# Attention and experts on one core: the opening's sums, softmax steps and load order are rearranged

## The chip, the core and the metric

One core of a Trainium2 chip runs the program. The metric is device time in microseconds (us), the median of several runs. An engine's instructions run in the order in which the program lists them; engines wait for each other by semaphores only. SP (SyncE) is a queue that issues transfers. TensorE is PE, and its weight loads are PEld; VectorE is DVE, ScalarE is ACT, GpSimd is POOL.

## What is computed

For 8 batches of 8 heads (576 tokens, 64 wide) a softmax of `phi` over 32 memory slots turns keys and values into 32 slots each; queries attend to them. The 4608 x 512 result goes to eight experts, one for each token.

```python
a = softmax(phi - max(phi))                  # over 32 slots
k_m = einsum('bhsm,bhsd->bhmd', a, k)        # and v_m with v
attn = softmax(q @ k_m.T / 8)
x = attn @ v_m                               # heads side by side: 512 wide
logits = x @ w_gate + modality_bias[modality_id]
e = argmax(logits)
out = gate_w * (relu(x @ w1[e]) @ w2[e])     # w1: 512 x 1024, w2: 1024 x 512
```

## The kernel before

The kernel guesses one expert for all tokens from the first token's modality, computes with that, and at the end tests whether a token wanted another. Every float32 operand of a long product is split into an upper and a lower part (names end in `h` and `l`), and three products of parts stand for one. The product of attention weights and values with `w1` is reordered: the 32 values of a head are multiplied with `w1` first (`vwh`, `vwl`, line 776), and attention weights (`xah`, `xal`) are multiplied with that (`hidden`, line 831); `outputs` (line 868) multiplies with `w2`.

This case is about batch 0's opening, all that runs before that stream of long products fills PE.

- `phi` of batch 0 comes in two halves, one from ACT's queue and one from SP's (lines 1331 and 1332). `first_max` (line 310) takes maxima on DVE, PE turns them, `mem_top` reduces them to `topc` (line 324). Four small DVE instructions (lines 219 to 225) choose the guessed expert; SP reads the number (line 226) and issues the loads of `w1` in two halves, `raw1`, with `load_rest` (small tables `mid` and `wg`) between them (lines 228 to 232).
- `mem_exp` subtracts the peak (DVE, line 375) and takes exponentials (ACT, line 378). `first_products` (line 433) multiplies them with keys and then with values on PE. DVE adds the exponentials up over the nine token columns meanwhile (lines 389 to 392), and eight small products (line 444) add over partitions.
- `first_divide` forms reciprocals (DVE, lines 453 to 457) and ACT scales the even heads (line 470); `first_odd` adds the odd ones (line 477); PE turns the keys (line 150, `first_keys`), which needs the product of values to be issued before it. `first_scores` (line 593) gives scores.
- Softmax goes by head groups g = 0 and 1: turn (line 624), max (628), subtract (630), exponential (632), sum and scaling (666 to 669), turn (673), then `first_split` makes `xah` (ACT, 679) and `xal` (DVE, 681).
- `value_products` multiplies values with the first half of `w1`, twice (line 776); `value_rest` subtracts the upper part from the second copy on PE (line 790). Then comes the second half of `w1` ("0, 1"), and then the products `ha` to `he` of `hidden` for the first four of eight 128-column pieces: `ha` needs `xah` of group 0, `hb` its `xal`, `hc` needs `vwl`, `hd` and `he` need group 1. The other four pieces and `outputs` follow.

`plan_first` lists these steps by hand. `weave` then merges the list with the experts' steps: it simulates time with the costs in `TAKES` (first number PE's us; D, A, P, T for the engines), takes the next listed step when what it depends on is done in that simulation, and takes experts' products otherwise. The listed order is kept, so a listed step that has to wait holds back all listed after it. At `("start",)` the simulated time is set to 25. `prepare` and `biases` (POOL, lines 271 to 286) work out the bias that `add_logits` (line 728) adds before `gate`; its result scales the output rows (line 881). POOL also forms the lower parts of `w2` (line 924).

Of the kernel before, what the change touches and what calls it, by code (L numbers as in the profile page):

```python
# [54 lines left out]
def attn_moe(ctx: ExitStack, tc: tile.TileContext, q, k, v, phi, mod_id, w_gate, mod_bias, w1, w2, out):  # L55
# [28 lines left out]
    BUSY = 64, 10  # L84
# [23 lines left out]
    places = const.tile([P, 2], F32, name="places")  # L108
    busy = const.tile([P, 512], BF16, name="busy")
# [112 lines left out]
    def guess():  # L222

        nc.vector.tensor_reduce(row[:, 0:1], live.pop("mine"), axis=AX.X, op=ALU.max)
        nc.vector.tensor_scalar(star, row[:, 0:1], -1.0, float(E), op0=ALU.mult, op1=ALU.add)
        e = nc.sync.value_load(star[0:1, 0:1], min_val=0, max_val=E - 1)
        first = w1[bass.ds(e, 1)].rearrange("a (c p) f -> (a p) c f", p=P)
        for hf in range(2):
            cols = slice(hf * 512, (hf + 1) * 512)
            nc.sync.dma_start(raw1[:, :, cols], first[:, :, cols])  # L230
            if hf == 0:
                load_rest()
        second = w2[bass.ds(e, 1)].rearrange("a (c p) d -> (a p) c d", p=P)
        raw = stage_pool.tile([P, W2N, DM], F32, name="raw2")
        nc.sync.dma_start(raw, second[:, 0:W2N])
        live["raw2"] = [raw[:, c] for c in range(W2N)]

        for c in range(W2N, FCH):
            if c < FCH - 1:
                raw = wk.tile([P, DM], F32, name="ob", bufs=2)  # L240
            else:
                raw = wk.tile([P, HG, 4 * M], F32, name="t2sums").rearrange("p h x -> p (h x)")
            nc.sync.dma_start(raw, second[:, c])
            live["raw2"].append(raw)
        load_queries(0, RA, RB)
        load_phi(1)

    def load_rest():
        nc.sync.dma_start(
            mid[0:QP].rearrange("p b c t -> p b (c t)"),  # L250
            mod_id.bitcast(I32).rearrange("(b p c t) -> p b (c t)", b=B, c=QC, t=2),
        )
        nc.sync.dma_start(wg, w_gate.rearrange("(a p) e -> p a e", p=P))
# [127 lines left out]
    def mem_sums(b):  # L381
        pe = live["pe", b][0]
        if b == 0:
            x = pe.rearrange("p j x -> p (j x)")
            n = QC // 3 * P
            t2 = wk.tile([P, HG, 4 * M], F32, name="t2top").rearrange("p j x -> p (j x)")[:, 0:n]
            r = wk.tile([P, HG, M], F32, name="sums", bufs=2)
            rf = r.rearrange("p j m -> p (j m)")
            nc.vector.tensor_tensor(t2, x[:, 0:n], x[:, n:2 * n], op=ALU.add)
            nc.vector.tensor_tensor(t2, t2, x[:, 2 * n:3 * n], op=ALU.add)  # L390
            nc.vector.tensor_tensor(rf, t2[:, 0:P], t2[:, P:2 * P], op=ALU.add)
            nc.vector.tensor_tensor(rf, rf, t2[:, 2 * P:3 * P], op=ALU.add)
            live["pe", b] = pe, r
            return
        live["pe", b] = pe, fold(nc.gpsimd, pe, ALU.add, "sums", "sums")
# [25 lines left out]
    def first_products(t):  # L421
# [5 lines left out]
        if t == 0:  # L427
            live["sums0"] = pk[:, :, 2 * D]
# [10 lines left out]
    def first_sums():  # L439
        sums = live["pe", 0][1]  # L440
        for g in range(NG):
            for j in range(0, HG, 2):
                half = slice(QP * g, QP * (g + 1))
                nc.tensor.matmul(
                    live["first", 0][g][M * j:M * (j + 2), 2 * D:2 * D + 1],
                    lhsT=sums[half, j:j + 2].rearrange("p j m -> p (j m)"), rhs=ones_c[half],
                    start=True, stop=True, tile_position=(QP * g, M * j),
                )
# [134 lines left out]
    def first_scores(c0, n):  # L583

        sc = [pair_of_banks(g) for g in range(NG)]
        qT = q_sb[0].rearrange("p j (c u t) -> p j c u t", u=2, t=BL)
        cs = slice(c0, c0 + n)
        for u in range(2):
            for j in range(HG):
# [21 lines left out]
    def soften(b, part, step=None, groups=None):  # L611
# [8 lines left out]
        for gs in groups_of(b, part) if groups is None else [slice(groups, groups + 1)]:  # L620
# [8 lines left out]
            if step in (None, 2):  # L629
                nc.vector.tensor_tensor(x, x, m.broadcast_to(list(x.shape)), op=ALU.subtract)  # L630
# [44 lines left out]
    def first_split(g, step):  # L675
        h, l = (x[:, 0, g].rearrange("p c x -> p (c x)") for x in xa)
        src = live["aT", 0][:, g, 0:RA * QP]
        if step == 0:
            nc.scalar.copy(h, src)
        else:  # L680
            nc.vector.tensor_tensor(l, src, h.bitcast(F32), op=ALU.subtract)
# [244 lines left out]
    def first_w2(c):  # L926
# [68 lines left out]
    def plan_first():  # L995
# [26 lines left out]
        add(("max", 0), "max0", [], first_max, floor=4.5)  # L1022
        add(("top", 0), "top0", [("max", 0)], mem_top, 0)
        add(("preferred",), "guess", [], preferred)
# [14 lines left out]
        add(("s", 0, 0), "s0", [("kT", 0), ("qt", 0, 0, 1)], first_scores, 0, RA)  # L1039
# [3 lines left out]
        add(("prepare",), "nothing", [], prepare)  # L1043
        add(("bias", 0), "nothing", [], biases, 0)
# [3 lines left out]
        for k in range(2):  # L1048
            add(("e", 0, 0, 1, k), "e1", [], soften, 0, 0, k, 1)
        add(("n", 0, 0, 0, 0), "n1", [("e", 0, 0, 0, 3)], first_weights, 0, 0)  # L1050
        add(("n", 0, 0, 0, 1), "n2", [], first_weights, 0, 1)
        add(("e", 0, 0, 1, 2), "e1", [], soften, 0, 0, 2, 1)
        add(("vw", 0, 0), "vwp", [("kvT", 0)], value_products, 0, 0, pair_(0))
        add(("vwu", 0, 0), "vwu", [("vw", 0, 0)], value_upper, 0)
        add(("vw", 0, 2), "vwp", [], value_products, 0, 0, None, True)
        add(("xu", 0, 0, 0), "xu1", [("n", 0, 0, 0, 1)], first_split, 0, 0)
        add(("e", 0, 0, 1, 3), "ee", [("e", 0, 0, 1, 2)], soften, 0, 0, 3, 1)
        add(("xl", 0, 0, 0), "e1", [("xu", 0, 0, 0)], first_split, 0, 1)
# [8 lines left out]
        add(("vwu", 0, 1, 0), "vw1", [("vw", 0, 1)], value_upper, 1, range(1))  # L1067
        add(("n", 0, 0, 1, 1), "n2", [], first_weights, 1, 1)
        add(("xu", 0, 0, 1), "xu1", [("n", 0, 0, 1, 1)], first_split, 1, 0)
        add(("vwu", 0, 1), "vw1", [("vw", 0, 1)], value_upper, 1, range(1, 2))  # L1070
# [9 lines left out]
        add(("s", 0, 1), "s1", [("qt", 0, 1, 1), ("vwl", 0, 1)], first_scores, RA, RB, floor=28.6)  # L1080

# [247 lines left out]
    with tc.manual_schedule():  # L1329
        mid0 = wk.tile([1, 2], I32, name="mid0")  # L1330
        for half, eng in ((slice(HG // 2, HG), nc.scalar), (slice(0, HG // 2), nc.sync)):
            eng.dma_start(phs[0][:, half], halves(phi, 0)[:, half])
# [11 lines left out]
        nc.gpsimd.memset(ones_c, 1.0)  # L1344
        ones_r = wk.tile([1, P], F32, name="ones_r")
# [138 lines left out]
```

## Time and profile before

| | us |
|---|---|
| median of 3 runs (lowest and highest) | 381.92 (380.41, 382.25) |
| the profiled execution, its own time | 380.38 |
| its span, first to last instruction | 378.6 |
| PE busy in it | 370.4 |
| DVE, ACT, POOL busy | 248.6, 139.7, 46.1 |

The span starts at 0; a row's first number is its start. An instruction's record on PE includes its depth in the pipeline, so records of successive products overlap, and the spacing of the starts is what counts.

### The profile page before, as it was taken

How to read it: one execution, taken by the hardware profiler on the slowest of the kernel's cores; microseconds unless marked ns; L12 is line 12 of the kernel's file. 1: busy time of each engine (PE TensorE's matmuls, PEld its weight loads, DVE VectorE, ACT ScalarE, POOL GpSimd, SP SyncE). 2: the span in 40 equal slices, each digit the busy share in tenths (PEclk: the TensorE clock that was granted, in tenths of full speed). 3: DMA queues.
4: the chain of work that ended last, by engine and by line, in shares of the span. 5: the costliest groups of instructions: out<-in, count | busy, mean ns of one | idle time of the engine just before them, and what ended most of it. 6: DMA issues, size and time to landing. Idle time of an engine off the chain costs nothing.

```text
span 378.6 us, 9983 instructions
## 1 busy us (share of the span) xinstructions
PE 370.4 (98%) x4045; PEld 308.5 (81%) x4045; DVE 248.6 (66%) x618; ACT 139.7 (37%) x328; POOL 46.1 (12%) x110
## 2 busy tenths in 40 slices
PE   6899999999999999999999999999999999999996
PEld 2677887889878898898987889797987979697986
DVE  4788758885958797868855689567874538750400
ACT  2382433524344054323415244431623306240401
POOL 3148030022130030004000030004000000000000
PEclk9999999999999999999999999999999999999999
DMA  8999668969969547583653737760232102321112
GB/s 290 348 377 239 110 121 250 292 114 304 282 113 287 216 72 141 155 311 61 110 167 99 270 70 128 214 205 2 56 110 74 29 2 55 119 64 30 30 35 56
DMA packets 93979, 56.89 MB, mean 150 GB/s; under 512 B 69732, under 2 KB 75108, under 8 KB 93924
## 3 DMA queue, kind: packets, MB, share of 16 engines
q1 hardware_dynamic: 93648, 55.87, 53.9%
q8 instruction: 33, 0.54, 0.6%
q10 hardware_dynamic: 276, 0.30, 0.2%
q14 instruction: 22, 0.18, 0.2%
HBM read 37.28 MB, written 18.87 MB: 148 GB/s over the span
## 4 chain that ended last, share of the span: by engine, by line
PE 88%; DVE 5%; DMA 3%; ACT 2%; issue 1%; SPq 1%; ACTq 0%; DVEq 0%
PE pe L868 48%; PE pe L831 26%; PE pair L408 4%; DMA raw<-in_moe_w_dram 2%; PE pe L776 2%; PE pair L571 2%; PE pe L912 2%; PE pair L776 1%; PE pair L713 1%; DMA ph<-in_phi_dram 1%; DVE vwl L156 1%; PE pair L150 1%; DVE top L310 1%; DVE a L650 0%; DVE sa L640 0%
## 5 line engine op out<-in xcount | busy, mean ns | idle before, releaser
L868 PE MATMUL pe<-w2h,hh 128*128 128x512 f32 x280 | 111.3, 397 | 0.0
L868 PE MATMUL pe<-w2h,hl 128*128 128x512 f32 x280 | 109.4, 391 | 0.0
L868 PE MATMUL pe<-w2l,hh 128*128 128x512 f32 x280 | 107.2, 391 | 0.0
L848 DVE SCALAR_TENSOR_TENSOR hl<-pe,hh 128x256 fp32r<-128x256 f32 (+2 forms) x158 | 56.7, 389 | 35.3 <-ACT hh L844 34.6
L844 ACT ACTIVATE hh<-pe 128x256 fp32r<-128x256 f32 (+2 forms) x158 | 52.5, 361 | 33.2 <-PE pe L831 32.6
L868 PEld LDWEIGHTS pe<-w2h,hh 128*128 128x128 f32 x280 | 52.6, 188 | 11.9 <-DVE vwl L156 0.8
L868 PEld LDWEIGHTS pe<-w2l,hh 128*128 128x128 f32 x280 | 52.5, 188 | 11.2
L868 PEld LDWEIGHTS pe<-w2h,hl 128*128 128x128 f32 x280 | 52.7, 188 | 9.8
L881 ACT ACTIVATE ob<-pe,gates 128x512 f32<-128x512 f32 x35 | 23.9, 688 | 68.6 <-PE pe L868 40.2
L831 PE MATMUL pe<-xbh,vwh 128*128 128x320 f32 x128 | 40.3, 314 | 0.1
L831 PE MATMUL pe<-xbh,vwl 128*128 128x320 f32 x128 | 39.6, 309 | 0.0
L831 PE MATMUL pe<-xbl,vwh 128*128 128x320 f32 x128 | 39.6, 309 | 0.0
L831 PE MATMUL pe<-xah,vwh 128*128 128x256 f32 x124 | 35.3, 287 | 0.4 <-DVE hl L848 0.4
L831 PE MATMUL pe<-xal,vwh 128*128 128x256 f32 x124 | 34.9, 283 | 0.0
L831 PE MATMUL pe<-xah,vwl 128*128 128x256 f32 x124 | 34.9, 283 | 0.0
L831 PEld LDWEIGHTS pe<-xah,vwh 128*128 128x128 f32 x124 | 23.6, 192 | 2.7 <-ACT vwl L793 0.8
L831 PEld LDWEIGHTS pe<-xbh,vwh 128*128 128x128 f32 x128 | 24.0, 188 | 1.4 <-issue 0.5
L344 POOL COPY ts<-tm 32x4 f32<-32x4 f32 x24 | 5.0, 210 | 165.2 <-DVE tm L336 164.4
L831 PEld LDWEIGHTS pe<-xbl,vwh 128*128 128x128 f32 x128 | 24.1, 188 | 0.3
L831 PEld LDWEIGHTS pe<-xbh,vwl 128*128 128x128 f32 x128 | 24.0, 188 | 0.0
L831 PEld LDWEIGHTS pe<-xal,vwh 128*128 128x128 f32 x124 | 23.7, 192 | 0.2
L831 PEld LDWEIGHTS pe<-xah,vwl 128*128 128x128 f32 x124 | 23.7, 192 | 0.0
(178 smaller groups left out, 465.5 us busy)
## 6 DMA issues: line engine op xcount, KB each, us to landing
out_dram<-ob SPq DMA_DIRECT2D x72, 128.0 KB, 2.4
q_sb<-in_q_dram SPq DMA_DIRECT2D x112, 72.0 KB, 3.1
kv_sb<-in_k_dram SPq DMA_DIRECT2D x6, 1152.0 KB, 6.4
kv_sb<-in_v_dram SPq DMA_DIRECT2D x6, 1152.0 KB, 9.2
ph<-in_phi_dram SPq DMA_DIRECT2D x13, 288.0 KB, 8.1
kv_sb<-in_k_dram SPq DMA_DIRECT2D x4, 576.0 KB, 5.6
kv_sb<-in_v_dram SPq DMA_DIRECT2D x4, 576.0 KB, 6.1
raw<-in_moe_w_dram SPq DMA_DIRECT2D x2, 1024.0 KB, 7.8
```

Source lines behind the costliest of these rows:

```text
L150: nc.tensor.transpose(dst, src, ident[:rows, :rows])
L156: nc.vector.tensor_tensor(l, src, h.bitcast(F32), op=ALU.subtract)
L344: nc.gpsimd.tensor_copy(ts_[BL * a:BL * (a + 1)], live["tm"][BL * o:BL * (o + 1)])
L408: nc.tensor.matmul(live["kvp"][M * j:M * (j + 1), g], lhsT=pe[half, j, c * M:(c + 1) * M], rhs=kv_sb[half, :, j, c * D:(c + 1) * D], start ...
L571: nc.tensor.matmul(sc[g][M * j:M * (j + 1), a, 0:QC * BL], lhsT=kvT[b][rows, 0, M * j:M * (j + 1)], rhs=qT[rows, j, a], start=True, stop=T ...
L776: nc.tensor.matmul(pvs[g][M * j:M * (j + 1), :], lhsT=vT[b][rows, j, :], rhs=raw1[rows, j, cols], start=True, stop=not more, tile_position ...
L831: nc.tensor.matmul(ph[:, 0:n], lhsT=(vl if k == 2 else vh)[:, g, cols], rhs=xl if k == 1 else xh, start=(g == k == 0), stop=(g == NG - 1 a ...
L844: nc.scalar.activation(hs[0][:, f, h0:h0 + p1 - p0], live["ph", f][:, p0:p1], AF.Relu)
L848: nc.vector.scalar_tensor_tensor(hl, live["ph", f][:, p0:p1], 0.0, hh.bitcast(F32), op0=ALU.max, op1=ALU.subtract)
L868: nc.tensor.matmul(po, lhsT=tile_columns(hl if n == 1 else hh, f, t), rhs=(w2l if n == 2 else w2h)[:, f, :], start=(f == n == 0), stop=(f ...
L881: nc.scalar.activation(ob, po, AF.Copy, scale=gate_of(b, t))
L912: nc.tensor.matmul(po, lhsT=x, rhs=w2s[w][:, f, cols], start=(f == i == 0), stop=(f == FCH - 1 and i == 2),)
```

## The change

- The order of the first loads: both halves of `phi` go out on SP's queue, before keys; ACT's queue starts with the first token's modality and the bias row.
- `load_rest` loses `wg` and leaves the place between the halves of `w1`; `wg` goes ahead of the next batch's `phi`, `mid` behind it.
- DVE's four additions and the eight small products go. Nine products on PE take their place (`first_sums`): each has 128 columns of exponentials as its weights and moves two columns (`groups`, zeros and ones).
- `preferred` (two of the four small DVE instructions) comes ahead of `mem_top`.
- `first_odd` comes ahead of both query turns; scores of batch 0 come in two steps, two heads each.
- The subtraction of group 1 and the forming of `xal` of group 0 move from DVE to POOL.
- The four products `ha` come ahead of the second half of `value_products`; group 1's weights stand earlier in the list than that half.
- `prepare` and `biases` move behind the last step on `w2`.
- 56 small warm-up products in place of 64.

```diff
-    BUSY = 64, 10
+    BUSY = 56, 10
+    groups = const.tile([P, NG], F32, name="groups")
 def guess():
             nc.sync.dma_start(raw1[:, :, cols], first[:, :, cols])
-            if hf == 0:
-                load_rest()
 ...
         load_queries(0, RA, RB)
+        nc.sync.dma_start(wg, w_gate.rearrange("(a p) e -> p a e", p=P))
         load_phi(1)
+        load_rest()
 def load_rest():
 ...
-        nc.sync.dma_start(wg, w_gate.rearrange("(a p) e -> p a e", p=P))
 def mem_sums(b):
-        if b == 0:
 ...
-            nc.vector.tensor_tensor(t2, x[:, 0:n], x[:, n:2 * n], op=ALU.add)
-            nc.vector.tensor_tensor(t2, t2, x[:, 2 * n:3 * n], op=ALU.add)
-            nc.vector.tensor_tensor(rf, t2[:, 0:P], t2[:, P:2 * P], op=ALU.add)
-            nc.vector.tensor_tensor(rf, rf, t2[:, 2 * P:3 * P], op=ALU.add)
 def first_products(t):
-            live["sums0"] = pk[:, :, 2 * D]
+            live["sums0"] = pk[:, 0, 2 * D:2 * D + NG]
 def first_sums():
-        for g in range(NG):
-            for j in range(0, HG, 2):
-                nc.tensor.matmul(live["first", 0][g][M * j:M * (j + 2), 2 * D:2 * D + 1], ...)
+        pe = by_rows(live["pe", 0][0])
+        for c in range(QC):
+            nc.tensor.matmul(
+                live["sums0"], lhsT=pe[:, c].rearrange("p j m -> p (j m)"), rhs=groups,
+                start=(c == 0), stop=(c == QC - 1),
+            )
 def first_scores(c0, n, js=range(HG)):
-            for j in range(HG):
+            for j in js:
 def soften(b, part, step=None, groups=None):
-                nc.vector.tensor_tensor(x, x, m.broadcast_to(list(x.shape)), op=ALU.subtract)
+                eng = nc.gpsimd if b == part == 0 and groups else nc.vector
+                eng.tensor_tensor(x, x, m.broadcast_to(list(x.shape)), op=ALU.subtract)
 def first_split(g, step):
-            nc.vector.tensor_tensor(l, src, h.bitcast(F32), op=ALU.subtract)
+            (nc.vector if g else nc.gpsimd).tensor_tensor(l, src, h.bitcast(F32), op=ALU.subtract)
 TAKES
-    "first sums": (0.0, "T1.9")     "s0": (0.75, "")
+    "ks0": (0.4, "")     "s0h": (0.4, "")     "e1p": (0.0, "P0.55")
 plan_first
+        add(("preferred",), "guess", [], preferred)
         add(("top", 0), "top0", [("max", 0)], mem_top, 0)
-        add(("preferred",), "guess", [], preferred)
 ...
-        add(("sums", 0), "first sums", [("exp", 0)], mem_sums, 0)
-        add(("ks", 0), "nothing", [("sums", 0)], first_sums)
-        add(("kn", 0), "kn0", [("k", 0), ("sums", 0)], first_divide)
+        add(("ks", 0), "ks0", [], first_sums)
+        add(("kn", 0), "kn0", [("ks", 0)], first_divide)
+        add(("ko", 0), "ko0", [("kn", 0)], first_odd, 0)
         turns(0, 0, 9.5)
-        add(("ko", 0), "ko0", [("kn", 0)], first_odd, 0)
         turns(0, 1, 11.0)
 ...
-        add(("s", 0, 0), "s0", [("kT", 0), ("qt", 0, 0, 1)], first_scores, 0, RA)
+        add(("s0", 0), "s0h", [("kT", 0), ("qt", 0, 0, 0)], first_scores, 0, RA, range(2))
+        add(("s", 0, 0), "s0h", [("s0", 0), ("qt", 0, 0, 1)], first_scores, 0, RA, range(2, HG))
 ...
-        add(("prepare",), "nothing", [], prepare)
-        add(("bias", 0), "nothing", [], biases, 0)
 ...
+        add(("n", 0, 0, 1, 0), "n1", [("e", 0, 0, 1, 3)], first_weights, 1, 0)
+        add(("n", 0, 0, 1, 1), "n2", [], first_weights, 1, 1)
+        some_hidden("ha", "h0c", [("xu", 0, 0, 0)], range(1), range(1))
         add(("vw", 0, 1), "vwp", [], value_products, 0, 1, pair_(0))
-        add(("n", 0, 0, 1, 0), "n1", [("e", 0, 0, 1, 3)], first_weights, 1, 0)
-        some_hidden("ha", "h0c", [("xu", 0, 0, 0)], range(1), range(1))
 ...
         add(("s", 0, 1), "s1", [("qt", 0, 1, 1), ("vwl", 0, 1)], first_scores, RA, RB, floor=28.6)
+        add(("prepare",), "nothing", [("w2", FCH - 1)], prepare)
+        add(("bias", 0), "nothing", [], biases, 0)
 the start of the program
-        for half, eng in ((slice(HG // 2, HG), nc.scalar), (slice(0, HG // 2), nc.sync)):
-            eng.dma_start(phs[0][:, half], halves(phi, 0)[:, half])
+        for half in (slice(0, HG // 2), slice(HG // 2, HG)):
+            nc.sync.dma_start(phs[0][:, half], halves(phi, 0)[:, half])
```

## Rows read from the trace of the kernel before

**Rows 1.** The page's first part: busy us of each engine, its share of the span, and instructions.

```profile
PE 370.4 (98%) x4045; PEld 308.5 (81%) x4045; DVE 248.6 (66%) x618; ACT 139.7 (37%) x328; POOL 46.1 (12%) x110
```

**Rows 2.** The chain of work that ended last, in order of time, its first 25 us. The columns are start, us, and what.

```profile
0.74 3.92 DMA ph<-in_phi_dram
...
4.68 2.18 DVE top L310 x2
...
7.33 0.29 DVE topc L324
...
8.29 0.47 DVE exp L375
...
11.41 8.40 DMA raw<-in_moe_w_dram
...
19.95 1.89 PE pair L776 x16
```

**Rows 3.** PE's products in order of time (start, us from the first start to the last end, line, out<-in, count; in brackets the idle time before and what ended it).

```profile
14.36 0.44 PE L150 MATMUL pair<-ident,keys 128*128 128x128 f32 x2
...
16.94 1.09 PE L776 MATMUL pair<-raw,kvT 64*32 64x512 f32 x16 [0.35 <-ACT kvT L539]
17.82 1.07 PE L776 MATMUL pe<-raw,kvT 64*32 64x512 f32 x16
18.82 0.94 PE L790 MATMUL pe<-vwh,minus 128*128 128x512 f32 x2
...
24.73 0.28 PE L831 MATMUL pe<-xah,vwh 128*128 128x256 f32 x1
```

**Rows 4.** PE's weight loads in order of time. 64*64 or 128*128 is the part of the array that is loaded (rows * columns).

```profile
8.73 0.29 PEld L258 LDWEIGHTS pair<-row,ones_r 1*128 1x128 f32 x2 [0.57 <-issue]
9.36 1.95 PEld L433 LDWEIGHTS pair<-kv_sb,exp 64*64 64x64 f32 x72 [0.33 <-ACT exp L378]
11.73 0.21 PEld L444 LDWEIGHTS pair<-ones_c,sums 64*64 64x64 f32 x8 [0.42 <-DVE sums L392]
11.84 1.72 PEld L433 LDWEIGHTS pe<-kv_sb,exp 64*64 64x64 f32 x59
13.77 0.42 PEld L433 LDWEIGHTS pe<-kv_sb,exp 64*64 64x64 f32 x13 [0.21 <-issue]
14.36 0.20 PEld L150 LDWEIGHTS pair<-ident,keys 128*128 128x128 f32 x2 [0.17 <-issue]
...
20.78 0.14 PEld L776 LDWEIGHTS pair<-raw,kvT 64*32 64x32 f32 x4 [0.67 <-issue]
```

**Rows 5.** PE's weight loads of the first 26 us, grouped by form: busy us and mean ns of one.

```profile
L258 PEld LDWEIGHTS pair<-row,ones_r 1*128 1x128 f32 x2 | 0.3, 184 | 0.6 <-issue 0.6
...
L150 PEld LDWEIGHTS pair<-ident,keys 128*128 128x128 f32 x2 | 0.2, 140 | 0.2 <-issue 0.2
```

**Rows 6.** DVE in order of time.

```profile
8.14 0.14 DVE L225 TENSOR_SCALAR star<-row 1x1 int32<-1x1 f32 x1
...
12.09 0.16 DVE L453 TENSOR_SCALAR den<-pair 128x2 f32<-128x2 f32 x1 [0.41 <-PE pair L444]
...
13.30 0.86 DVE L477 SCALAR_TENSOR_TENSOR keys<-pair,recs,even 128x64 f32<-128x64 f32 x4
...
20.52 0.42 DVE L681 TENSOR_TENSOR xal<-aT,xah 128x256 fp32r<-128x256 f32 x1
...
21.63 0.42 DVE L669 TENSOR_TENSOR a<-a,ra 128x256 f32<-128x256 f32 x1
...
33.89 0.96 DVE L630 TENSOR_TENSOR a<-a,mx 128x640 f32<-128x640 f32 x1
```

**Rows 7.** ACT in order of time.

```profile
20.08 0.41 ACT L679 CAST xah<-aT 128x256 fp32r<-128x256 f32 x1 [0.87 <-DVE aT L673]
```

**Rows 8.** Stretches of one us: from, to, its length, then busy us and instructions of PE, PEld, DVE, ACT and POOL, the granted TensorE clock, the busy share of the 16 DMA engines, GB/s.

```profile
14.00:15.00 1.00, 0.80 (x16) 0.39 (x8) 0.78 (x2) 0.16 (x1) 0.00 (x0) 1.00 1.27 217
...
19.00:20.00 1.00, 0.82 (x8) 0.28 (x12) 0.93 (x4) 0.21 (x1) 0.92 (x3) 1.00 1.03 375
```

**Rows 9.** Transfers issued in the first 5 us: queue, size, us from issue to landing.

```profile
ph<-in_phi_dram ACTq DMA_DIRECT2D x1, 288.0 KB, 4.2
ph<-in_phi_dram SPq DMA_DIRECT2D x1, 288.0 KB, 3.9
```

**Rows 10.** POOL in order of time, the first 50 us.

```profile
17.09 0.35 POOL L271 CAST mid_f<-mid 64x16 f32<-64x16 int32 x2 [9.68 <-DMA mid<-in_moe_modality_id_dram]
...
19.82 0.34 POOL L286 TENSOR_TENSOR bias<-bias,part 128x72 f32<-128x72 f32 x1
...
32.86 1.31 POOL L924 TENSOR_TENSOR w2l<-ob,w2h 128x512 fp32r<-128x512 f32 x1
34.12 1.89 POOL L924 TENSOR_TENSOR w2l<-t2sums,w2h 128x512 fp32r<-128x512 f32 x1
...
49.75 0.74 POOL L299 TENSOR_TENSOR t2sums<-t2sums 128x256 f32<-128x256 f32 x1
```

**Rows 11.** The chain that ended last, 40 to 44 us.

```profile
40.77 0.19 DVE lg L728
...
42.45 0.70 ACT ob L881
...
43.19 0.85 PE pe L831 x4
```

More of the change, by code (lines that the diff above doesn't have):

```diff
@@ L382, in mem_sums @@
         pe = live["pe", b][0]
-        if b == 0:
[L384 to L388, printed above, removed]
-            nc.vector.tensor_tensor(t2, x[:, 0:n], x[:, n:2 * n], op=ALU.add)
-            nc.vector.tensor_tensor(t2, t2, x[:, 2 * n:3 * n], op=ALU.add)
-            nc.vector.tensor_tensor(rf, t2[:, 0:P], t2[:, P:2 * P], op=ALU.add)
-            nc.vector.tensor_tensor(rf, rf, t2[:, 2 * P:3 * P], op=ALU.add)
-            live["pe", b] = pe, r
-            return
         live["pe", b] = pe, fold(nc.gpsimd, pe, ALU.add, "sums", "sums")
@@ L439, in first_sums @@
     def first_sums():
-        sums = live["pe", 0][1]
-        for g in range(NG):
-            for j in range(0, HG, 2):
[L443 to L448, printed above, removed]
+        pe = by_rows(live["pe", 0][0])
[4 more added lines that the diff above has]
+            )
     def first_divide():
@@ L581, in scores, with first_scores @@
             load_queries(b + 2)
-    def first_scores(c0, n):
-        sc = [pair_of_banks(g) for g in range(NG)]
+    def first_scores(c0, n, js=range(HG)):
+        sc = [pair_of_banks(g) for g in range(NG)] if js[0] == 0 else live["sc", 0]
         qT = q_sb[0].rearrange("p j (c u t) -> p j c u t", u=2, t=BL)
@@ L1049, in plan_first @@
             add(("e", 0, 0, 1, k), "e1", [], soften, 0, 0, k, 1)
+        add(("e", 0, 0, 1, 2), "e1p", [("e", 0, 0, 1, 1)], soften, 0, 0, 2, 1)
         add(("n", 0, 0, 0, 0), "n1", [("e", 0, 0, 0, 3)], first_weights, 0, 0)
         add(("n", 0, 0, 0, 1), "n2", [], first_weights, 0, 1)
-        add(("e", 0, 0, 1, 2), "e1", [], soften, 0, 0, 2, 1)
         add(("vw", 0, 0), "vwp", [("kvT", 0)], value_products, 0, 0, pair_(0))
         add(("vwu", 0, 0), "vwu", [("vw", 0, 0)], value_upper, 0)
+        add(("e", 0, 0, 1, 3), "ee", [("e", 0, 0, 1, 2)], soften, 0, 0, 3, 1)
         add(("vw", 0, 2), "vwp", [], value_products, 0, 0, None, True)
         add(("xu", 0, 0, 0), "xu1", [("n", 0, 0, 0, 1)], first_split, 0, 0)
-        add(("e", 0, 0, 1, 3), "ee", [("e", 0, 0, 1, 2)], soften, 0, 0, 3, 1)
-        add(("xl", 0, 0, 0), "e1", [("xu", 0, 0, 0)], first_split, 0, 1)
+        add(("xl", 0, 0, 0), "e1p", [("xu", 0, 0, 0)], first_split, 0, 1)
         add(("vwr", 0, 0), "vwr", [("vwu", 0, 0)], value_rest, 0)
@@ L1061, in plan_first @@
             add(("vwl", 0, 0, g), "vw1", [("vwr", 0, 0)], value_remainder, 0, g)
+        add(("n", 0, 0, 1, 0), "n1", [("e", 0, 0, 1, 3)], first_weights, 1, 0)
+        add(("n", 0, 0, 1, 1), "n2", [], first_weights, 1, 1)
+        some_hidden("ha", "h0c", [("xu", 0, 0, 0)], range(1), range(1))
         add(("vw", 0, 1), "vwp", [], value_products, 0, 1, pair_(0))
-        add(("n", 0, 0, 1, 0), "n1", [("e", 0, 0, 1, 3)], first_weights, 1, 0)
-        some_hidden("ha", "h0c", [("xu", 0, 0, 0)], range(1), range(1))
         some_hidden("hb", "h0c", [("xl", 0, 0, 0)], range(1, 2), range(1))
         some_hidden("hc", "h0c", [("vwl", 0, 0, 0)], range(2, 3), range(1))
-        add(("vwu", 0, 1, 0), "vw1", [("vw", 0, 1)], value_upper, 1, range(1))
-        add(("n", 0, 0, 1, 1), "n2", [], first_weights, 1, 1)
         add(("xu", 0, 0, 1), "xu1", [("n", 0, 0, 1, 1)], first_split, 1, 0)
-        add(("vwu", 0, 1), "vw1", [("vw", 0, 1)], value_upper, 1, range(1, 2))
+        for g in range(NG):
+            add(("vwu", 0, 1, g) if g == 0 else ("vwu", 0, 1), "vw1", [("vw", 0, 1)], value_upper, 1, range(g, g + 1))
         add(("w2", 0), "w2", [], first_w2, 0)
@@ L1344, in attn_moe @@
         nc.gpsimd.memset(ones_c, 1.0)
+        for g in range(NG):
+            for r in range(NG):
+                nc.gpsimd.memset(groups[QP * r:QP * (r + 1), g:g + 1], float(g == r))
         ones_r = wk.tile([1, P], F32, name="ones_r")
```

4 rows, old and new, of the table TAKES are left out of this document.

## The prediction

> **What bounds the kernel now.** The page's first part comes first [rows 1]: PE is busy in 370.4 of 378.6 us, so a change pays only where PE waits, and most of that is in the opening. The chain of waits, in order of time, says what the opening is made of [rows 2]: `phi` lands at 4.66, DVE takes maxima until 6.86, `topc` ends at 7.62, the first subtraction starts at 8.29, and the second half of `w1` lands at 19.81, upon which PE starts that half's products at 19.95. That last link invites a misreading. In PE's order of time the product before it ends at 18.82 + 0.94 = 19.76 [rows 3], so the load costs PE 0.19 us and no more; a second chain, through softmax, arrives just as late. `xah` of group 0 is ready at 20.08 + 0.41 = 20.49 [rows 7]. From 19.95 PE is dense: 16 products with `w1` and 24 of `hidden` until, at 24.73, the other four pieces begin [rows 2, 3]. I take 24.73 as the mark: behind it PE runs products back to back, and what the mark moves, the end moves.
>
> **Front of the opening: 0.6 us gained.** The two halves of `phi` now come one behind the other on one queue. They landed at 0.74 + 3.9 and 0.73 + 4.2 [rows 9], sharing the engines, and both maxima waited for the first. Alone, the first should land earlier by about half of what the other half adds; DVE needs 2.18 / 2 = 1.09 for each [rows 2], so the second half has that long to come. I take 0.5. Bounds: nothing (both still land at 4.65), and 0.9 (the second half lands at 4.9, and 4.9 + 1.09 = 6.0 in place of 6.86). `preferred` moves into PE's turn of the maxima, and only `guess` stays between `topc` and the subtraction, beside PE's spreading of the peak. Of the 8.29 - 7.62 = 0.67 us there [rows 2] most is that spreading; I take 0.1, between nothing and 0.3. `preferred` is a new wait ahead of `mem_top` on DVE, for the modality's bias; that came behind half of `phi` on ACT's queue and now comes first, so I book nothing; if it were late, the 0.5 would go.
>
> **The sums: 1.4 us lost.** The additions that go are on DVE, not on PE. From the first load for keys at 9.36 to the first for values at 11.84 PE's load stream takes 2.48 [rows 4]: 72 loads in 1.95, a wait of 0.42 for DVE's sums, eight small loads in 0.11. Wait and small loads go: -0.53. In their place stand nine float32 products of two passes each, the two instructions that line 258 also shows for one product, so 18 loads of the whole 128 x 128 array. No row shows such a stream; the nearest: 64 x 64 loads come 1.95 / 72 = 0.027 apart [rows 4], and one whole array is four of them, 0.108; line 258's two loads of 128 columns take 0.29 together and 0.184 each, so 0.11 apart [rows 4, 5]. These agree, and I take 18 x 0.107 = 1.93. Low end: the two turns of keys load 128 x 128 at 0.20 together and 0.140 each, 0.06 apart [rows 4, 5], which gives 1.08; the planner's own cost in the diff, 0.4, is lower still. I stay with line 258, since its two loads are passes of one ordinary product and a turn is another instruction. So -0.53 + 1.93 = +1.4 (low ends +0.55 and -0.13).
> The Trainium skill weighs in on the other side: "TensorE: Matmul & The Clock Gate", Back-to-back issue gap, puts products of up to 64 columns at about 25 ns each once the clock is up. By that alone 18 take an estimated 0.45 and the step would be a small gain; line 258's spacing speaks against it, and its own case is below.
>
> What waits for it: `first_divide` starts later (12.09 before [rows 6]), but the turn of the keys at 14.36 [rows 3] comes behind the products of values on PE, and these behind the sums. DVE's keys are done at 13.30 + 0.86 = 14.16 [rows 6], and `first_odd` ahead of the query turns only makes that earlier, so PE's order decides. Everything from the keys' turn to `xah` shifts by -0.6 + 1.4 = +0.8. The query turns (0.7 each) now come behind keys on DVE and end before the scores they feed; splitting the scores adds no product: nothing for both.
>
> **Softmax on POOL: nothing on the path.** Group 1's subtraction and group 0's `xal` take 0.74 on POOL each (its 128 x 256 row [rows 10]) against 0.42 on DVE [rows 6]. `xah` of group 0 doesn't pass through either. DVE gets group 1 done some 0.9 earlier, but the products that need it come after 20 others. The new wait is of `hb` for POOL's `xal`: `xah` + 0.74, and PE is in the second half's products by then. If that cover were gone, it would cost 0.3.
> DVE and POOL are not free of each other: POOL's last step on `w2` takes 1.89 in place of 1.31 beside DVE's subtraction at 33.89 [rows 6, 10]. The Trainium skill, "SBUF — State Buffer", SBUF: two separate sides, calls it an exclusive lock between a two-input DVE instruction and a GpSimd one; that row agrees. Here it can hold group 1's scaling (21.63 before [rows 6]) for half a us, and that has slack.
>
> **Four products ahead: 1.4 us later, 0.8 us back.** `ha` waits for `xah`: 20.49 + 0.8 = 21.29, so PE starts at about 21.34 what it started at 19.95: +1.39. The load no longer matters: without the tables the second half of `w1` lands earlier, as the stretch with the small packets moves 217 GB/s where 375 is usual [rows 8]; that gain is lost in the wait. The dense work behind is the same 4.78 us (24.73 - 19.95) less one thing. The second half's 16 products took 1.89, the 16 at 16.94 and at 17.82 1.09 and 1.07 [rows 2, 3]; four of their loads came at 20.78 after 0.67 us in which PE waited for nothing shown [rows 4]. The like happens at 13.77 (0.21). I read it as instructions not yet fetched, while the DMA engines are full [rows 8]; in the changed kernel PE comes to this place over 1 us later, after a wait, so I expect the 0.82 to go. Mark: 21.34 + 4.78 - 0.82 = 25.30, +0.57.
>
> **Later: 0.15 us lost.** `prepare` and `biases` took 17.09 to 20.16 on POOL, 3.07 us, and now follow `w2` there, from 36.01 [rows 10]. With the shift they end at about 39.7; `add_logits` wants the bias at 40.77 + 0.6 [rows 11]. What they cost DVE by contention on the way to the gates, which release PE at 43.19 [rows 11], I put at 0.15, between nothing and 0.8. The planner holds back batch 0's listed steps until it thinks `w2` done; on DVE nothing else stands between them, so the logits' product moves behind one more product on PE (0.23), within its slack. Eight warm-up products less, four small fills more, SP's loads of `phi`: beside the wait for `phi`, nothing.
>
> **Sum.** +0.57 + 0.15 = +0.7. The profiled execution took 380.38 and would take 381.1; it lies 1.54 under the median of the runs, so the forecast is 381.92 + 0.7 = 382.6.
>
> **Rivals.**
> - *The sums are cheap.* For it: the keys' turns, and the planner's 0.4. Against it: line 258. With 0.4, everything shifts by -0.6 - 0.13 = -0.73, `ha` starts at 19.81, the mark is 19.81 + 4.78 - 0.82 = 23.77: -0.96 + 0.15 = -0.8, so 381.1; with 1.08 it is -0.1. With the front's best, -1.4.
> - *The pause comes back.* It follows the instruction stream rather than the clock on the wall, and PE pays 0.82 again: +1.5, so 383.4. For it: it happened twice in 7 us; against it: the longer wait ahead.
> - *The bias comes too late* (the other side). It decides once POOL ends its nine small instructions over 1.7 us later than reckoned (41.4 less 39.7). Each can be held by DVE as the `w2` step was, 0.58; all nine would be 5.2, so PE's release slips by 3.5 and the end by +4.2: 386.1. Against it: DVE has few two-input instructions there.
> - *It does nothing*: the terms cancel within 0.3; part of the first and second cases.
>
> **Numbers.** Forecast 0.45 (own range 381.8 to 383.4), cheap sums 0.25, the pause 0.20, late bias 0.06, others 0.04. A measurement of this kernel tells about 0.5%, 1.9 us, from no change. No case but the late bias reaches that at its own value; the runs spread by -1.5 and +0.3 around their median, which with the ends of the first rival gives 0.07 for faster, and with the ends of the pause's case 0.11 for slower: 0.82 for no change. The range goes from cheap sums with a good front, 380.5, to the pause with a poor front, 383.9.
>
> **What would show it.** Right: the first maximum starts near 4.2; the new loads of the sums stand about 0.107 apart and take 1.9 us; the keys' turn starts near 15.2; PE idles some 0.8 us ahead of `ha`, which starts near 21.3; the second half of `w1` releases nothing; its 16 products take 1.1. Wrong: sums in under 1.1 us, `ha` before 20.5, four late loads again, or DVE waiting for the bias.

## The result: 383.82 us, 0.8% slower than before

| | before | after |
|---|---|---|
| median of 9 runs on one chip (lowest, highest) | 380.55 (380.01, 382.25) | 383.82 (382.99, 385.83) |
| the profiled execution, its own time | 380.38 | 383.66 |
| its span | 378.59 | 381.87 |
| the mark (first product of the second four pieces) | 24.73 | 28.24 |
| span less mark | 353.86 | 353.63 |

The ratio is 1.0083, 95% interval 1.0066 to 1.0100. (Here and below a ratio leaves single disturbed runs out and need not be the quotient of the two medians.) The time lies in the range, at its upper end, 1.2 above the forecast, and it is slower by more than the 0.5% that the prediction took for the least difference a measurement can tell. Everything happened ahead of the mark: +3.51 there, -0.23 behind it. PE's busy time grew from 370.4 [rows 1] to 373.1:

```profile
PE 373.1 (98%) x4047; PEld 312.6 (82%) x4047; DVE 246.7 (65%) x612; ACT 139.7 (37%) x328; POOL 48.2 (13%) x116
```

The chain of work that ended last answers to [rows 2]: start, us, what.

```profile
1.75 7.99 DMA kv_sb<-in_k_dram
...
9.87 3.50 PE pair L421 x72
13.38 2.41 PE pair L430 x18
15.79 2.13 PE pe L421 x72
...
23.62 0.41 ACT xah L665
...
24.07 0.50 PE pe L817 x2
```

It no longer starts with `phi` and the maxima but with keys. PE's weight loads, beside [rows 4] (here the brackets give the idle time before and what ended it):

```profile
9.84 3.13 PEld L421 LDWEIGHTS pair<-kv_sb,exp 64*64 64x64 f32 x72 [1.42 <-ACT known L259]
13.30 2.39 PEld L430 LDWEIGHTS pair<-groups,exp 128*128 128x128 f32 x18 [0.33 <-issue]
15.71 1.95 PEld L421 LDWEIGHTS pe<-kv_sb,exp 64*64 64x64 f32 x72
17.84 0.24 PEld L151 LDWEIGHTS pair<-ident,keys 128*128 128x128 f32 x2 [0.17 <-issue]
```

Keys' 72 loads took 3.13 in place of 1.95. The one-us windows, with the columns of [rows 8], say why: the seventh number is the granted clock.

```profile
8.00:9.00 1.00, 0.42 (x3) 0.29 (x2) 1.00 (x3) 0.84 (x2) 0.00 (x0) 1.00 1.06 376
9.00:10.00 1.00, 0.13 (x4) 0.16 (x8) 0.05 (x1) 0.67 (x3) 0.00 (x0) 1.00 1.01 392
10.00:11.00 1.00, 1.00 (x33) 1.00 (x36) 0.00 (x0) 0.00 (x0) 0.00 (x0) 0.79 1.04 367
11.00:12.00 1.00, 1.00 (x27) 1.00 (x23) 0.00 (x0) 0.00 (x0) 0.00 (x0) 0.50 1.07 370
...
13.00:14.00 1.00, 1.00 (x12) 0.69 (x4) 0.00 (x0) 0.00 (x0) 0.00 (x0) 0.50 1.08 414
14.00:15.00 1.00, 1.00 (x11) 1.00 (x11) 0.00 (x0) 0.00 (x0) 0.00 (x0) 1.00 1.03 387
```

It fell to half, TensorE's lower level (1.2 of 2.4 GHz), between 10 and 14, just as PE's work began after nearly two us of little. In the profile of before the column says 1.00 throughout the opening. DVE, ACT (first in the kernel before, then in the changed one) and POOL, against [rows 2, 6, 10]:

```profile
3.82 2.18 DVE L310 TENSOR_REDUCE top<-ph 128x64 f32<-128x576 f32 x2 [3.82 <-DMA ph<-in_phi_dram]
...
7.57 1.48 DVE L375 TENSOR_TENSOR exp<-ph,pe 128x384 f32<-128x384 f32 x3 [0.36 <-PE pe L368]
...
24.16 0.96 DVE L655 TENSOR_TENSOR a<-a,ra 128x256 f32<-128x256 f32 x1
```

```profile
8.78 1.45 ACT L378 ACTIVATE exp<-exp 128x384 f32<-128x384 f32 x3 [5.04 <-DVE exp L375]
```

```profile
8.16 1.45 ACT L378 ACTIVATE exp<-exp 128x384 f32<-128x384 f32 x3 [5.01 <-DVE exp L375]
```

```profile
24.10 0.74 POOL L667 TENSOR_TENSOR xal<-aT,xah 128x256 fp32r<-128x256 f32 x1 [1.33 <-DMA raw<-in_moe_w_dram]
...
42.25 0.34 POOL L286 TENSOR_TENSOR bias<-bias,part 128x72 f32<-128x72 f32 x1
```

The first maximum starts at 3.82 (before 4.68), the subtraction at 7.57 (8.29), and ACT's first exponential at 8.16 (before 8.78): the front gained 0.6 to 0.7 as forecast. The bias is done at 42.59, ahead of the logits. From the mark's side, PE beside [rows 3]:

```profile
24.07 0.50 PE L817 MATMUL pe<-xah,vwh 128*128 128x256 f32 x2 [0.74 <-ACT xah L665]
...
24.74 1.09 PE L762 MATMUL pair<-raw,kvT 64*32 64x512 f32 x16
...
28.24 0.28 PE L817 MATMUL pe<-xah,vwh 128*128 128x256 f32 x1
```

PE waits 0.74 for `xah`, `ha` follows, and the second half of `w1` takes 1.09 without the pause. The difference, stretch by stretch (start to start, from these rows and the named ones):

| stretch | before | after | difference | forecast |
|---|---|---|---|---|
| to ACT's first exponential | 8.78 | 8.16 | -0.62 | -0.6 |
| from there to keys' first load | 0.58 | 1.68 | +1.10 | 0 |
| first load for keys to first for values | 2.48 | 5.87 | +3.39 | +1.4 |
| values, to the keys' turn | 2.52 | 2.13 | -0.39 | 0 |
| keys' turn to the mark | 10.37 | 10.40 | +0.03 | -0.23 |
| mark to the end | 353.86 | 353.63 | -0.23 | +0.15 |
| sum | | | +3.28 | +0.7 |

### The profile page after: what moved, and what is told of

It is laid out like the page before. It is cut to its first block, busy times and chain, and to the rows that moved or that the text cites. A ratio compares the mean times of both kernels' runs of the same rounds, so it can differ in the third digit from the quotient of the medians.

```text
span 381.9 us, 9986 instructions
## 1 busy us (share of the span) xinstructions
PE 373.1 (98%) x4047; PEld 312.6 (82%) x4047; DVE 246.7 (65%) x612; ACT 139.7 (37%) x328; POOL 48.2 (13%) x116
## 4 chain that ended last, share of the span: by engine, by line
PE 90%; DVE 5%; DMA 2%; ACT 2%; issue 1%; SPq 0%; ACTq 0%; DVEq 0%
PE pe L854 47%; PE pe L817 26%; PE pair L396 4%; PE pe L762 2%; PE pair L556 2%; DMA kv_sb<-in_k_dram 2%; PE pe L898 2%; PE pair L699 1%; PE pair L762 1%; PE pair L421 1%; DVE vwl L157 1%; PE pair L430 1%; PE pair L151 1%; PE pair L578 1%; PE pe L421 1%
```

## The experiments

Three explanations stood against each other, under letters that come back in the expectations: K, both halves of `phi` on SP's queue make keys land late, PE waits for them, and the clock falls for that wait; C, the low clock is what costs, and PE kept busy there keeps it up; S, the nine products of the sums are most of it by themselves. Of every run I give the median, the ratio to the kernel before on the same chip with its interval, and what the profiled execution shows.

### Keys: one queue or two

The changed kernel with `phi` on two queues (`e1_phi_two_queues`):

```diff
-        for half in (slice(0, HG // 2), slice(HG // 2, HG)):
-            nc.sync.dma_start(phs[0][:, half], halves(phi, 0)[:, half])
+        for half, eng in ((slice(HG // 2, HG), nc.scalar), (slice(0, HG // 2), nc.sync)):
+            eng.dma_start(phs[0][:, half], halves(phi, 0)[:, half])
```

> The changed kernel, with the second half of phi back on ACT's queue as before; all else as changed. Theory K (keys): with both halves of phi ahead of them on one queue the keys land at 9.74 in place of 7.96, PE waits 1.35 us for them, and the granted clock falls behind that wait. Then here keys land near 8, the first maximum starts near 4.7, keys' products start near 9.3, the clock stays at 1.00, the new sums take 1.9 us and the products of values start near 13.1 (15.7 in the changed kernel): about 2.3 us faster than the changed kernel, 1.0 slower than before. Rival R (keys late for another reason, or by chance): keys near 9.7, wait and low clock stay, time as the changed kernel. By theory S alone (only the sums cost) at most 0.5 us off the changed kernel.

The kernel before with both halves on SP's queue, the same edit the other way round (`e2_before_phi_one_queue`):

> The kernel before, with both halves of phi on SP's queue and nothing else changed. Theory K: keys land near 9.7, keys' products start near 9.9 (9.36 before) after a wait of over 1 us, the granted clock falls to 0.5 behind it and these products take about 3.5 us (2.2 before); the products of values start near 13.4 in place of 11.84. The mark (second four pieces, 24.73 before) comes 0.6 to 1.6 us later, and so does the end. Rival R: keys near 8, products of keys start a little earlier than 9.36, time within 0.5 us of before.

Measured: 384.43, ratio 1.0078 (1.0056 to 1.0101), and 382.98, 1.0054 (1.0034 to 1.0074); before on that chip 380.46. Issue to landing of keys, in before, in the changed kernel on two queues, in before on one (the changed kernel: 7.99, in its chain above):

```profile
kv_sb<-in_k_dram SPq DMA_DIRECT2D x1, 1152.0 KB, 6.7
```

```profile
kv_sb<-in_k_dram SPq DMA_DIRECT2D x1, 1152.0 KB, 6.3
```

```profile
kv_sb<-in_k_dram SPq DMA_DIRECT2D x1, 1152.0 KB, 8.7
```

K's first half is shown in both directions: 6.3 to 6.7 with two queues, 8.0 and 8.7 with one, and the edit alone makes the kernel before half a per cent slower. Its second half, that the clock falls for the wait, fell twice. In the kernel before with one queue PE waited 2.37 for keys, and their products then ran at the full clock, 2.19 (K expected 3.5):

```profile
10.56 2.19 PE L433 MATMUL pair<-kv_sb,exp 64*64 64x128 f32 x72 [2.37 <-DMA kv_sb<-in_k_dram]
```

The low clock came there from 18 to 25, behind a pause of 1.92 in values, and this profiled execution, 385.23, is above its median. And in the changed kernel with keys in time the clock fell all the same, with no wait for keys ahead:

```profile
9.09 3.30 PEld L421 LDWEIGHTS pair<-kv_sb,exp 64*64 64x64 f32 x72 [0.31 <-ACT exp L378]
```

```profile
8.00:9.00 1.00, 0.78 (x4) 0.29 (x2) 1.00 (x3) 0.48 (x2) 0.00 (x0) 1.00 1.03 410
9.00:10.00 1.00, 0.91 (x26) 0.91 (x29) 0.41 (x1) 1.00 (x4) 0.00 (x0) 0.79 1.03 398
...
12.00:13.00 1.00, 1.00 (x18) 0.67 (x10) 0.00 (x0) 0.00 (x0) 0.00 (x0) 0.50 1.07 401
```

Its median was no lower than the changed kernel's, as eight of its twelve runs had a mean clock of 0.991 or less, against three of nine. At an equal mean clock it was about 0.5 faster: 384.3 to 384.7 against 384.8 to 385.8 at 0.991, 383.0 and 383.2 against 383.0 to 384.2 at 0.996. That is a fifth of the 2.3 that K expected.

Why one queue brings keys 1.8 later, when they are issued only 0.5 later, was not settled: the DMA engines are busy in both.

### The wait filled

The changed kernel with eight wide fill products in place of two, in PE's wait for the exponentials and keys (`e4_filled_wait`):

```diff
-        nothing(2)
+        nothing(8)
```

> The changed kernel with eight 512-column products of zeros in place of two, just ahead of the products of keys, so that PE is busy while it waits for keys (6 x 0.215 = 1.3 us more); nothing waits for them. Theory C: the low clock from 10.8 to 14.0 comes from the wait, and costs 1.3 us in the products of keys and 0.46 in the sums. Here the clock stays at 1.00, products of keys take 2.2, the sums 1.93, and the time is 1.8 us under the changed kernel. Rival: the clock falls all the same, or its cost is made up for later: time as changed.

Measured 382.95, ratio 1.0061 (1.0038 to 1.0084): 2.5 over before on its chip, where the changed kernel is 3.3 over. The clock stayed at 1.00 and keys' loads took 1.98, the sums' 2.08:

```profile
10.32 1.98 PEld L421 LDWEIGHTS pair<-kv_sb,exp 64*64 64x64 f32 x72 [0.40 <-ACT known L259]
12.48 2.08 PEld L430 LDWEIGHTS pair<-groups,exp 128*128 128x128 f32 x18 [0.17 <-issue]
```

```profile
11.00:12.00 1.00, 1.00 (x47) 1.00 (x40) 0.00 (x0) 0.00 (x0) 0.00 (x0) 1.00 1.08 395
```

Half the gain expected came: keys started at 10.32 in place of 9.84, and values had a pause of 0.29. So C is a part, and a fill can keep the clock. Both cures together (`e6_two_queues_filled`) were to give 381.6:

> The changed kernel with phi's second half back on ACT's queue, and eight wide fill products in place of two in PE's wait ahead of the exponentials. Theory KC (late keys and a fallen clock both cost, and each cure works when the other is there): keys land near 7.6, keys' products start near 9.1, take 2.2, the clock stays at 1.00; the filled run went from keys' products (10.36) to its mark (27.58) in 17.2, so mark 26.3, span 380.0, 381.6 us. Rival C (the clock falls whatever stands ahead, as it did with two queues): keys' products 3.6, mark 27.5, 384.4 as in that run. Rival N (early keys are worth nothing behind the exponentials): as the filled run, 383.0.

They gave 384.22, ratio 1.0090 (1.0068 to 1.0113). In the profiled execution the clock was at 0.50 from 8 to 11, and the eight fills, 0.43 apart in place of 0.22, held up keys themselves until 12.02:

```profile
8.28 3.34 PE L162 MATMUL pair<-busy 128*128 128x512 bf16 x8
...
12.02 1.21 PE L421 MATMUL pair<-kv_sb,exp 64*64 64x128 f32 x36
```

The time is rival C's (384.4), the way is not: keys and sums ran at the full clock here, behind the fills. None of the three theories had this: a fill in front of work that is due costs its own time when the clock is low.

### The sums

The changed kernel with the old sums (`e3_sums_on_dve`); then the same with ten warm-up products more, so that PE's instructions stand where they did (`e5_dve_sums_stream`):

```diff
+        if b == 0:
+            ...
+            nc.vector.tensor_tensor(t2, x[:, 0:n], x[:, n:2 * n], op=ALU.add)
+            ...
-        for c in range(QC):
-            nc.tensor.matmul(live["sums0"], lhsT=pe[:, c].rearrange("p j m -> p (j m)"), rhs=groups, ...)
+        for g in range(NG):
+            for j in range(0, HG, 2):
+                ...
```

> The changed kernel with the sums as before (four additions on DVE and eight small products); all else as changed. Theory S: the 18 whole-array loads stand on PE's path with all their 2.4 us, so the products of values start near 13.2 in place of 15.7 and the time is 2.3 us under the changed kernel, 0.7 to 1.0 over before (keys still late, clock still low). If PE's sums were not on the path, the time stays as changed.

> The changed kernel with the old sums (DVE's additions, eight small loads) and ten warm-up products more, so that behind the sums every PE instruction has the number that it has in the changed kernel; the run with the old sums alone had ten load-and-product pairs less and two pauses of 1.9 and 1.2 us far behind the mark. Theory F (those pauses hang on where the stream of instructions stands when it is fetched): the span less the mark is 353.7 +- 0.3 again in place of 356.6, the mark 27.3 as in that run, so a span of 381.0 and 382.8 us, 2.9 under that run and 1.0 under the changed kernel; that 1.0 is what the sums on PE cost net. Rival D (DVE's additions or the shape of the old sums did it): 356.6 and 385.7 again. Rival W (the sums on PE cost nothing): mark 28.2, 383.8.

Measured: 385.66, ratio 1.0126 (1.0101 to 1.0150), and 382.33, 1.0054 (1.0035 to 1.0072). The mark of the first was 27.29, near a us better, but its span less mark was 356.59, 2.9 too long. PE's two pauses there, in brackets, "issue" meaning that nothing shown was waited for:

```profile
115.30 0.21 PE L416 MATMUL pair<-ones_c,sums 64*32 64x1 f32 x5 [1.82 <-issue]
```

```profile
292.36 0.22 PE L416 MATMUL pair<-ones_c,sums 64*32 64x1 f32 x6 [1.06 <-issue]
```

Both are at products of a later batch that the edit does not touch. With the stream put back they are gone, and span less mark is 353.5: theory F holds, in that the pauses hang on the length of the stream. That PE waits there for instructions not yet fetched is not shown by an edit, but the traces fit it. Each such pause ends 2.2 to 2.6 us after a 16 KB packet starts on the DMA queue that the profile calls "instruction": here the packets start at 112.66 and 289.99, and in the kernel before at 11.45 and 18.35, for the pauses that end at 13.77 and 20.78 [rows 4]. The clean comparison is the second run, with its mark at 26.73: it is 2.0 over before's 380.32, so taking the sums from PE gives back 1.3 us of the 3.3, net of what the clock does with and without them (five of its six runs are at 0.996). Seen from the changed kernel S, most of it by the sums alone, falls.

From the other side, the kernel before with nothing but the sums on TensorE (`e8_before_sums_on_pe`, ten warm-up products fewer; `e10_sums_on_pe_warm`, all 64):

> The kernel before with the sums on TensorE as in the change, nothing else of it (ten warm-up products fewer, so that the stream behind the sums stands as before). Theory S (18 loads of 128 columns take 1.9 to 2.2 at the full clock, 1.4 to 1.7 more than what goes): from the first load for keys to the first for values 3.9 to 4.2 in place of 2.48; the second half of w1 then waits for PE and not for its load, so the mark moves by 1.2 to 1.5, to 26.0 to 26.2, and the time to 381.9; 0.8 less if the pause in that half goes. Rival cheap sums: 0.4 for them, mark 24.7, 380.5. Rival C (the clock falls by them): over 383.

> The kernel before with the sums on TensorE as in the last such run, but with all 64 small warm-up products (there 54). That run had five of six runs at a mean clock of 0.990 to 0.994 (382.3 to 383.8) and one at 1.000 (380.6). Theory U (fewer warm-up products let the clock fall later): at least half of the runs near 1.000, as of before, and a median near 381. Rival S (the clock falls because of the sums, or by chance): 0.990 to 0.996 in most runs, median 382.5 to 383.5. At the clock of 1.000 both expect 380.6, 0.7 above the runs of before at 1.000 (379.9).

Measured: 383.04, ratio 1.0071 (1.0050 to 1.0093), and 382.72, 1.0042 (1.0020 to 1.0064). The first one's profile is of its one run at a mean clock of 1.000 (380.60):

```profile
9.08 1.95 PEld L422 LDWEIGHTS pair<-kv_sb,exp 64*64 64x64 f32 x72 [0.34 <-ACT exp L379]
11.20 2.08 PEld L431 LDWEIGHTS pair<-groups,exp 128*128 128x128 f32 x18 [0.17 <-issue]
13.30 1.95 PEld L422 LDWEIGHTS pe<-kv_sb,exp 64*64 64x64 f32 x72
```

This is the price of the sums without the clock: 18 loads in 2.08, 0.116 apart, and 4.22 from keys to values, +1.74. The mark was 25.52, only 0.79 later: keys started 0.28 sooner, values had no pause (-0.39), and from the keys' turn to the mark it took 10.09 (-0.28), without the pause in `w1` but with a wait of 0.51 for `xah` of group 1. The other five runs, at 0.990 to 0.994, took 382.3 to 383.8. With all warm-up products 8 of 12 were at 0.996 or lower, so it is not their number alone that decides (theory U falls), and in the profile the low stretch lay elsewhere, behind the sums, in values:

```profile
13.61 3.30 PEld L422 LDWEIGHTS pe<-kv_sb,exp 64*64 64x64 f32 x72
```

Put into the kernel before, the sums alone thus cost 2.7 by the medians (383.04 against 380.32), and the one queue alone 2.5; both with all the rest of the change cost 3.3. The shares do not add up, and the clock is only part of the reason. At mean clocks alike (0.994 to 0.996) the one queue costs the kernel before some 2.4 (382.6 to 383.4 against 380.3 to 380.8), where it cost the changed kernel 0.5; the profile of before with one queue also shows a wait of 0.70 for values and the pause of 1.92. How often these come in its other runs is not shown.

### What is left of the change

Two queues and the old sums, stream aligned (`e7_neither`); then also `ha` behind the second half of `w1`, as before (`e9_ha_behind`):

```diff
-        some_hidden("ha", "h0c", [("xu", 0, 0, 0)], range(1), range(1))
         add(("vw", 0, 1), "vwp", [], value_products, 0, 1, pair_(0))
+        some_hidden("ha", "h0c", [("xu", 0, 0, 0)], range(1), range(1))
```

> The changed kernel without its two suspects: phi on two queues and the sums on DVE, with ten warm-up products more so that the stream stands as in the changed kernel. Left of the change: small tables fetched later, preferred ahead, softmax steps on POOL, four products ahead, the bias later. Theory (the prediction's terms without the sums): the front as with two queues, xah no later than before (20.5), ha at 20.5, mark 24.73 + 0.55 - 0.82 = 24.5, span 378.2, about 380.3 us, no different from before (380.5). Rival C (the clock falls at the keys' products): 1.2 more, mark 25.7, 381.5. Rival P (POOL's steps or the late bias cost by themselves): the span less the mark above 354.

> The run with phi on two queues and the sums on DVE, with one thing more put back: the four products ha stand behind the second half of w1 again, so that PE has 16 products to do while xah is made. Theory H (the four products ahead cost PE a wait for xah of 0.6 to 0.9 that the second half used to fill, and what they gave back in the profile was only a pause for instructions that the kernel before doesn't always have): the turn of the keys to the mark takes 9.6 to 10.1 in place of 10.43, and the time falls by 0.3 to 0.8 from 381.1, to 380.3 to 380.8, level with before. Rival P (the pause comes back with the old order, as in the profile of before): 10.4, 381.1. Rival G (the four ahead gain, as the prediction had it): over 381.5.

Measured: 381.12, ratio 1.0027 (1.0014 to 1.0039), and 382.10, 1.0031 (1.0012 to 1.0050). The first is 0.8 over before, so the two suspects together hold some 2.5 of the 3.3; the 380.3 expected did not come. Its profile is rival C's case, mark 25.70, the low clock again from 9 to 13:

```profile
9.28 3.40 PEld L433 LDWEIGHTS pair<-kv_sb,exp 64*64 64x64 f32 x72 [0.31 <-ACT exp L378]
12.62 0.48 PEld L444 LDWEIGHTS pair<-ones_c,sums 64*64 64x64 f32 x8
12.95 2.03 PEld L433 LDWEIGHTS pe<-kv_sb,exp 64*64 64x64 f32 x72
```

DVE's sums are ready before PE is, and the wait of 0.42 in [rows 4] is gone: part of what the clock costs is hidden there, as it cannot be when PE makes the sums. What the 0.8 that is left comes from stays open: the runs at a mean clock of 0.999 or 1.000 (380.9 to 382.2) are no faster than the three at 0.994 to 0.996 (381.1 to 381.3). In the second, at full clock, the turn of the keys to the mark took 9.76 (10.43 in the first):

```profile
15.01 0.44 PE L151 MATMUL pair<-ident,keys 128*128 128x128 f32 x2
...
20.43 1.38 PE L777 MATMUL pair<-raw,kvT 64*32 64x512 f32 x16
21.74 0.51 PE L832 MATMUL pe<-xah,vwh 128*128 128x256 f32 x2
...
24.77 0.28 PE L832 MATMUL pe<-xah,vwh 128*128 128x256 f32 x1
```

So H is right on the stretch: PE filled its wait for `xah` with the second half, and no pause of 0.82 came. The median did not follow: 7 of its 12 runs had a mean clock of 0.996 or less (381.6 to 382.7), against 3 of 12 of the first, and the profiled one, 380.59, lost 1.14 to a pause in values that the first did not have:

```profile
14.41 0.42 PEld L433 LDWEIGHTS pe<-kv_sb,exp 64*64 64x64 f32 x15 [1.14 <-issue]
```

### The kernel before, again, and kept busier

> The kernel before, unchanged, once more, for a second profile on this chip. If its runs at a mean clock of 1.000 (379.5 to 380.2) lack the pause of 0.82 ahead of the mark, its mark is 24.0 to 24.3; if the clock is 0.995, the low stretch shows where it lies and what it costs (0.5 by the medians). With pause and full clock: 24.7 again.

One run, 382.07, mark 26.74. PE's warm-up and keys (`e11_before_again`), and the window 11 to 12:

```profile
2.08 4.43 PE L161 MATMUL pair<-busy 128*128 128x512 bf16 x10
...
10.12 4.12 PE L433 MATMUL pair<-kv_sb,exp 64*64 64x128 f32 x72
```

```profile
11.00:12.00 1.00, 1.00 (x28) 1.00 (x24) 0.93 (x3) 0.00 (x0) 0.00 (x0) 1.00 1.05 348
```

Ten wide products in 4.43, 0.427 apart to the last; 512 columns in 0.427 us are the lower level, 1.2 GHz. In the first profile of before they come 0.22 apart from 5.0 on, and the ten take 3.85. Here keys' products too took 4.12 in place of 2.20, although the column says 1.00. It says so too in both profiles for the first wide products, 0.43 apart: where the clock is low from the first product on, the column shows no fall, and the spacing is the surer sign. The kernel before is not free of it either: three of its 23 other runs beside this one lie at 381.9 to 382.3 with a mean clock of 0.999, so a mean near 1.000 does not show that the opening ran at the full clock. Last, three wide products more in the kernel before (`e12_before_busier`):

```diff
-    BUSY = 64, 10
+    BUSY = 64, 12
-        nothing(2)
+        nothing(3)
```

> The kernel before with three wide products more that compute nothing: twelve at the start in place of ten, three in place of two in the wait ahead of the exponentials. In the profiles of before PE is idle from 5.9 to 7.0, and in the second one the wide products stay 0.43 apart to the end and the keys' 72 loads take 3.7 in place of 1.95. Theory L (the idle stretch is what keeps the clock low in part of the runs): fewer runs at 0.995 or above 381.5, keys' loads 1.95, median 379.7 to 380.1, under before's. Rival R (when the clock rises is a matter of the run, whatever stands there): the same mixture, 380.3 to 380.6. Rival D (in runs with the low clock the three delay the turn of the maxima and the row's products by up to 0.4 each): 380.8 or more.

Measured 380.05 against 379.97, ratio 0.9991 (0.9977 to 1.0005): not faster. But its 12 runs lie from 379.73 to 380.46, all at a mean clock of 0.999 or 1.000, where the 17 runs of before beside them go from 379.64 to 381.97, four of them at 0.991 to 0.995. No run shows the low stretch, which is theory L's first half, and the median gained nothing:

```profile
2.08 3.98 PE L161 MATMUL pair<-busy 128*128 128x512 bf16 x12
...
9.16 2.20 PE L433 MATMUL pair<-kv_sb,exp 64*64 64x128 f32 x72
```

## Why the prediction was right, and where not

**The range held the time by luck; the account under it did not hold.** The forecast was +0.7, the profiles show +3.28; the case that came, slower by over 0.5%, had a chance of 0.11. The sum was laid on 381.92, the median of three runs of before; the nine runs beside the changed kernel have 380.55. As a change the range went from -1.4 to +2.0, and the +3.27 of the medians lies outside it. Of the signs named for being right, those of single steps came (PE idle 0.74 ahead of `ha`, nothing released by the second half of `w1`, 1.09 for its products); those of the sum did not: the loads of the sums took 2.39, the keys' turn started at 17.84 and `ha` at 24.07.

- *Front, -0.6*: right, -0.62.
- *The step that failed: "SP's loads of `phi`: beside the wait for `phi`, nothing".* That holds for the issue, but not for what lies behind it on the queue. Keys stand third there instead of second, landed at 9.74 in place of 7.96, and PE waited for them: +1.10, the whole front and more. The prediction followed `phi`'s move on ACT's queue, to the modality's bias, but not on SP's, to keys. No rival held it.
- *The clock, not in the sum at all.* At the full clock keys to values takes 4.22 with the sums on PE; the changed kernel took 5.87, so 1.65 is the clock's in that profile. That the clock can fall in the opening was not considered, as the one profile of before showed 1.00 throughout; all nine runs of the changed kernel show 0.991 or 0.996. That a filled wait can keep it up is shown (4 of 6 runs at 1.000), though with `phi` on two queues only 1 of 5 was; that the wait is needed for the fall is refuted by the changed kernel on two queues. What sets how often it falls in each kernel stays open.
- *The sums, +1.4*: nearly. 18 loads were put at 0.107 and 1.93, and took 2.08 at the full clock in four kernels; with the gap ahead of them (0.17) the stretch grew by 1.74. The neighbour chosen, line 258, was the right one. The Trainium skill's 25 ns for short products ("TensorE: Matmul & The Clock Gate", Back-to-back issue gap) is the gap of a product by itself; the same section has the spacing of load-and-product pairs set by both. With a whole-array load for each the runs show 116 ns; PE's loads are busy through the whole of that stretch.
- *Values* got 0.39 back: the pause of 0.21 in [rows 4] did not come in the changed kernel. Such pauses came and went from kernel to kernel (0.29, 0.66, 0.79, 1.14, 2.17 in the loads of the same place in other kernels).
- *`ha` ahead, and the pause that goes*: right in kind. PE idled 0.74 (0.8 forecast), the load of `w1` released nothing, the pause was absent: the 16 KB packet ahead of it started at 20.19, and 2.4 us later PE was still over 2 us short of that half. In size it was a draw, +0.03 (-0.23 forecast): the pause that went paid for the wait that came. The run with `ha` behind shows a better order.
- *POOL*: right. DVE's scaling of group 1 took 0.96 in place of 0.42 while POOL made `xal`, 24.10 to 24.84; it held nothing on the path. These rows agree with the lock that the Trainium skill states ("SBUF — State Buffer", SBUF: two separate sides).
- *Later, +0.15*: -0.23; the bias came in time.

The rival nearest in time, the pause's return (383.4), is not what happened: the pause stayed away.

## What to carry to other kernels

When a transfer is moved on a queue, follow every transfer behind it to its first consumer, with the landing times of the trace: what the front gained was lost on the next load. In a latency-bound opening look at the spacing of products of known width in more than one execution before counting on the full clock, and take it at both levels in the range. And when an edit removes or adds instructions, put the stream back to the same length before reading its time.

## What was not expected of the hardware

- Pauses of PE with nothing waited for, of 1.8 and 1.1 us, some 100 and 280 us behind an edit that made the stream of instructions shorter; restoring its length alone took them away (356.6 to 353.5 behind the mark).
- The clock's first rise differs from run to run in one and the same kernel: at about 5 us in one profile of before, not ahead of 13 in the other. The Trainium skill says the like of one kernel's count of slow products ("TensorE: Matmul & The Clock Gate", Part 1: The HAM clock gate), and this trace agrees. Here it cost 2.0 in the mark, 24.73 to 26.74.
- A transfer of 1152 KB, third instead of second on its queue and issued 0.5 later, landed 1.8 later.
